# A tuned attention and mixer-MLP kernel: the second FFN product by seven block products, in groups of 256 tokens

## Chip, cores and metric

One core of a Trainium2 chip. The metric is device time in microseconds (us). Fast runs of the kernel before, on one chip, differ by up to 1.4 per cent here (265.68 to 269.4 in one set); short stretches at half TensorE clock, which the traces show, are at least part of the reason. Medians are over all runs, slow ones included (one of four in runs 8, 13 and 15, two of four in runs 1 and 7, three of four in run 14). Ratios are the mean time of one kernel's fast runs over the mean of the other's fast runs of the same rounds, so they are not quite the ratios of the medians quoted beside them. Faster or slower needs 2 per cent.

## The reference, cut to what matters

Block attention (4 batches, 8 heads, 768 tokens, 64 numbers a head; keys and values are first mixed over blocks by a matrix) gives `x` of 768 x 512 for each batch. Then a token-mixing and a channel-mixing layer follow:

```python
a1 = alpha1 * x + beta1
tok = np.einsum('ts,bsd->btd', w_tok, a1)
u = x + lam * tok
a2 = alpha2 * u + beta2
ch = np.maximum(a2 @ w_ch1, 0.0) @ w_ch2     # 512 -> 2048 -> 512
return u + lam * ch
```

`w_ch2` is called W2 below, and `np.maximum(...) @ w_ch2` is the second FFN product. `lam` is a vector over the 512 output channels.

## The kernel before

A batch is worked in two halves of 384 tokens. For each half the first product (`h_ps`) goes in 16 pieces, then the second (`ch_ps`) in three tiles of 128 tokens. While one half multiplies, the attention of the next batch is slotted between the pieces, by a table of places. Each engine gets its work in the order in which the program writes it. Some words of this text: the *affine* is `alpha * x + beta` ahead of a mixing layer (tiles `a` and `a2T`); *turned* means transposed by TensorE (`qt_ps`, then `qT`); *tails* are copies into the last 32 rows of a tile of 128 tokens, as a block has 96; a *pitch* is the time from one matmul's start to the next one's; the *return* is the reading back of values into `Vs`.

```python
def h_part(b, hf, m, cis):
    ...
        h_of[m] = psb([128, 384], FT, "h_ps")          # one of 4 PSUM buffers
    ...
        act.activation(hT_of[(b, hf)][m], h_of[m][:], AF.Relu)

def ch_unit(b, hf, kk, part=(0, HT)):
    ...
    for m in range(*part):                             # 16 matmuls of 512 columns
        pe.matmul(cps[:, 0:w], hT[m][:, kk * 128:(kk + 1) * 128], W2p[:, m, 0:w], ...)
    ...
    dve.tensor_tensor(ost[:], cps[:], lamB[:], ALU.mult)
    (dve if b == B - 1 and hf == 1 else pool).tensor_tensor(ost[:], ost[:], u_of[b][kt], ALU.add)
    act_out(out[b, kt * 96:(kt + 1) * 96, :], ost[0:96, :])

def moe_tok(b, kt, ps):                                # lam here: two operations on VectorE, one on GpSimd
    ...
    dve.tensor_tensor(tmp[:], tok_of[(b, kt)][:], lamB[:], ALU.mult)
    dve.tensor_tensor(u16_of[b][:, kt, :], tmp[:], x_of[b][:, kt, :], ALU.add)
    (pool if b else dve).tensor_tensor(u32[kt], tmp[:], x_of[b][:, kt, :], ALU.add)
```

The values of a later batch are mixed, written to memory (`vscr`) and read back in another order into `Vs`; there were two `Vs` buffers.

The softmax here doesn't subtract the row's maximum and nothing guards it: scores larger than these inputs give would overflow.

## Time and profile before

| | before |
|---|---|
| time, median of 3 | 265.45 us (265.23 to 265.5) |
| profiled run | 268.76 us, span 267.0, with 10.2 us at half clock from 22.8 us on |
| busy: TensorE, VectorE, ScalarE, GpSimd | 96, 57, 50, 38 per cent |

The profiled run is 3.3 us longer than the timed ones. It has one stretch at half clock in the head, which ends at 33 us. I take this for the cause, so from there on its places in time lie some 3.3 us later than in a typical run. The prediction shows the page's lines. The one view of before that it does not show is the timeline of GpSimd at 72 us (start, duration, engine, operation, count, idle time ahead of it and what ended that), which also belongs here:

```profile
74.54 1.26 POOL L65 TENSOR_TENSOR ost<-ost,u 128x512 f32<-128x512 f32 x1 [1.18 <-DVE ost L65]
75.75 1.11 POOL L65 DMA_DIRECT2D raw<-in_v_dram  x2
```

GpSimd issues batch 2's loads (`raw`, values first) only after its third add of `u` to an output tile.

### The profile page before, as it was taken

What the parts mean: (1) busy time and instruction counts of PE and PEld (TensorE: products, weight loads), DVE (VectorE), ACT (ScalarE), POOL (GpSimd) and SP (SyncE); (2) the same over time, 40 slices, a digit from 0 to 9 for tenths busy, and PEclk for the clock granted to TensorE, in tenths of its full rate; (3) what the DMA queues carried; (4) which work ended last, traced back from release to release, by engine and by line L of the source; (5) the groups of instructions that cost most, each with busy time, mean ns of one, the idle gap of its engine ahead of it and who ended that gap; (6) DMA issues with size and microseconds to landing.
All of it is one profiled execution on the core that took longest, in us unless ns stands there. A gap on an engine that the chain in (4) does not pass through costs nothing.

```text
span 267.0 us, 5344 instructions
## 1 busy us (share of the span) xinstructions
PE 256.0 (96%) x2148; PEld 142.7 (53%) x2164; DVE 151.4 (57%) x333; ACT 133.0 (50%) x238; POOL 100.8 (38%) x109
## 2 busy tenths in 40 slices
PE   8987899999999999999999999999999999999993
PEld 3465766454655545555465455555565445545552
DVE  5767567797729995434978453415794554121032
ACT  3675457344497539565257189474363014505600
POOL 8882600901184055629610444601301746031000
PEclk9997599999999999999999999999999999999998
DMA  6999999996959976996994348911110332112012
GB/s 99 204 210 196 206 206 214 169 143 150 147 120 202 136 137 148 148 140 121 177 166 91 60 96 185 153 24 39 43 39 0 61 90 68 21 39 79 0 42 79
DMA packets 67368, 31.03 MB, mean 116 GB/s; under 512 B 56640, under 2 KB 63056, under 8 KB 67344
## 3 DMA queue, kind: packets, MB, share of 16 engines
q0 software_dynamic: 26352, 15.34, 41.3%
q1 hardware_dynamic: 40896, 15.29, 30.3%
q8 instruction: 17, 0.28, 0.4%
q10 hardware_dynamic: 96, 0.07, 0.1%
q14 instruction: 7, 0.06, 0.1%
HBM read 32.78 MB, written 8.65 MB: 155 GB/s over the span
## 4 chain that ended last, share of the span: by engine, by line
PE 82%; DMA 6%; DVE 5%; POOL 2%; issue 2%; ACT 1%; SPq 0%; DVEq 0%; ACTq 0%; POOLq 0%
PE h_ps L65 29%; PE ch_ps L65 27%; PE tok_ps L65 12%; PE x_ps L65 4%; DMA v<-in_v_dram 3%; DMA out_dram<-ost 3%; PE sc_ps L65 3%; DVE a L65 2%; PE v_ps L65 2%; PE kmix_ps L65 2%; PE mix_ps L65 1%; DVE ost L65 1%; PE wtok_ps L65 1%; POOL vd L65 1%; DVE Vs L65 1%
## 5 line engine op out<-in xcount | busy, mean ns | idle before, releaser
L65 PE MATMUL h_ps<-a2T,W1p 128*128 128x384 bf16 x512 | 92.0, 326 | 0.4 <-DVE ost L65 0.3
L65 ACT ACTIVATE hTa<-h_ps 128x384 bf16<-128x384 f32 x96 | 46.7, 493 | 54.6 <-PE h_ps L65 54.4
L65 PE MATMUL ch_ps<-W2p,hTa 128*128 128x512 bf16 (+1 forms) x285 | 67.5, 370 | 0.8
L65 PEld LDWEIGHTS <-W1p 128*128 128x128 bf16 x512 | 48.3, 98 | 32.7 <-issue 0.8
L65 POOL TENSOR_TENSOR ost<-ost,u 128x512 f32<-128x512 f32 x21 | 26.6, 1267 | 77.3 <-DVE ost L65 59.2
L65 DVE TENSOR_TENSOR ost<-ch_ps,lamB 128x512 f32<-128x512 f32 (+1 forms) x25 | 16.7, 669 | 50.3 <-PE ch_ps L65 47.1
L65 PEld LDWEIGHTS <-hTa 128*128 128x128 bf16 x300 | 28.4, 98 | 28.9
L65 POOL TENSOR_TENSOR u<-toktmp,x 128x512 f32<-128x512 f32 x18 | 29.6, 1650 | 33.7 <-DVE toktmp L65 33.7
L65 ACT ACTIVATE et<-sc_ps 96x768 f16<-96x768 f32 (+1 forms) x32 | 25.0, 810 | 21.2 <-PE sc_ps L65 21.2
L65 PE MATMUL tok_ps<-a,w_tokT 128*128 128x512 f16 x126 | 30.3, 379 | 0.1
L65 ACT CAST kT<-kmix_ps 64x512 f16<-64x512 f32 x32 | 22.9, 717 | 10.1 <-PE kmix_ps L65 9.8
L65 DVE TENSOR_TENSOR toktmp<-tok_ps,lamB 128x512 f32<-128x512 f32 x21 | 14.5, 690 | 21.1 <-PE tok_ps L65 21.1
L65 PE MATMUL ch_ps<-W2p,hTb 128*128 128x512 bf16 (+1 forms) x99 | 24.6, 371 | 0.1
L65 PEld LDWEIGHTS <-w_tokT 128*128 128x128 f16 x126 | 12.3, 98 | 14.0 <-DVE a L65 0.5
L65 ACT ACTIVATE hTb<-h_ps 128x384 bf16<-128x384 f32 x32 | 15.7, 490 | 7.5 <-PE h_ps L65 7.2
L65 DVE TENSOR_TENSOR u<-toktmp,x 128x512 f16<-128x512 f32 (+1 forms) x24 | 17.0, 718 | 0.7
L65 POOL DMA_DIRECT2D qn<-in_q_dram x18 | 16.0, 929 | 3.5 <-DMA raw<-in_v_dram 3.5
L65 DVE TENSOR_TENSOR x<-x_ps,rcb 96x512 f16<-96x512 f32 x24 | 16.5, 687 | 0.8
L65 DVE TENSOR_SCALAR a2T<-uT,ab2col 128x384 bf16<-128x384 f16 x28 | 9.7, 409 | 11.2 <-DMA uT<-u 9.1
L65 PEld LDWEIGHTS <-et 96*128 96x128 f16 (+4 forms) x288 | 13.0, 106 | 5.3 <-issue 1.2
L65 PE MATMUL x_ps<-Vs,et 96*128 96x65 f16 (+4 forms) x288 | 14.2, 203 | 1.3 <-ACT et L65 0.9
L65 PEld LDWEIGHTS <-hTb 128*128 128x128 bf16 x100 | 9.5, 98 | 9.7
(114 smaller groups left out, 235.7 us busy)
## 6 DMA issues: line engine op xcount, KB each, us to landing
out_dram<-ost SPq DMA_DIRECT2D x23, 192.0 KB, 2.4
raw<-in_v_dram POOLq DMA_DIRECT2D x6, 384.0 KB, 7.6
raw<-in_k_dram POOLq DMA_DIRECT2D x6, 384.0 KB, 9.1
qn<-in_q_dram POOLq DMA_DIRECT2D x18, 128.0 KB, 10.0
vscr<-mixed SPq DMA_DIRECT2D x6, 384.0 KB, 4.6
Vs<-vscr SPq DMA_DIRECT2D x3, 768.0 KB, 7.9
W1p<-in_moe_w_ch_dram POOLq DMA_DIRECT2D x4, 512.0 KB, 13.0
W2p<-in_moe_w_ch_dram POOLq DMA_DIRECT2D x4, 512.0 KB, 14.1
```

Source lines behind the costliest of these rows:

```text
L65: ins = getattr(self.eng, name)(*args, **kwargs)
```

## The change

The intent: seven products of half-size blocks in place of eight (Strassen's scheme) save an eighth of the second product's matmul columns. For this, tokens go in three groups of 256, so that the hidden matrix splits into 2 x 2 blocks; W2 and the hidden values become fp16; VectorE makes four sums of hidden blocks per group and, once, four sums of W2's blocks; a product is accumulated over others in PSUM and copied out in between by ScalarE. The token affine carries `lam` (times 1024), so token mixing needs one VectorE operation. `Vs` has one buffer. The core of the diff, cut:

```diff
-            hTa = moep.tile([128, 12, 384], BF, name="hTa", tag="hTa", bufs=1)
+            hT_of[(b, g)] = moep.tile([128, HP, 2, GS], F16, name="hT", tag="hT", bufs=1)   # GS = 256
...
+    def sums(b, g, lo, hi, which):              # VectorE: 88 operations of 128x512 fp16 in all
+            dve.tensor_tensor(S[n], *((A[1][0], A[1][1]), (S[0], A[0][0]), (A[0][0], A[1][0]), (A[0][1], S[1]))[n], ...)
...
+        if n == 0:
+            product(b, g, 1, range(HP - 1))     # each product: 8 matmuls of 256 columns
+            product(b, g, 2, range(3))
+            product(b, g, 1, range(HP - 1, HP))
+            act.copy(o0[:, lo_c], a())
+            sums(b, g, 4, HP, (0, 1))
+        elif n == 1:
+            product(b, g, 2, range(3, HP))
+            dve.tensor_tensor(o0[:, lo_c], o0[:, lo_c], half(0), ALU.add)
+            sums(b, g, 4, HP, (2, 3))
+        elif n == 2:
+            product(b, g, 6, range(HP))         # accumulates on product 1: waits for the copy
+            act.copy(o0[:, hi_c], a())
+        elif n == 3:
+            product(b, g, 5, range(HP))
+            act.copy(ch_of["r"][:], half(1))
...                                             # products 7, 3, 4 likewise
+            dve.tensor_tensor(o[:, c], o[:, c], lamB[:, c], ALU.mult)
+            (dve if last else pool).tensor_tensor(o[:, c], o[:, c], u_of[(b, kt)][:, c], ALU.add)
...
-        dve.tensor_tensor(tmp[:], tok_of[(b, kt)][:], lamB[:], ALU.mult)
-        dve.tensor_tensor(u16_of[b][:, kt, :], tmp[:], x_of[b][:, kt, :], ALU.add)
-        (pool if b else dve).tensor_tensor(u32[kt], tmp[:], x_of[b][:, kt, :], ALU.add)
+        dve.scalar_tensor_tensor(u, tok_of[(b, kt)][:], 1.0 / LIFT, x_of[b][:, kt, :], op0=ALU.mult, op1=ALU.add)
+        act.copy(u16_of[b][:, kt, :], u)
...
-    Vs = [const([128, H * NB, GRP], F16, f"Vs_{n}") for n in range(2)]
+    Vs = const([128, H * NB, GRP], F16, "Vs")
```

The table of places was written anew for groups of 256; the very first group stays plain.

## The prediction

> **What bounds the kernel now.** I read the page first: the busy shares, then the slices.
>
> ```profile
> PE 256.0 (96%) x2148; PEld 142.7 (53%) x2164; DVE 151.4 (57%) x333; ACT 133.0 (50%) x238; POOL 100.8 (38%) x109
> ...
> PE   8987899999999999999999999999999999999993
> ...
> PEclk9997599999999999999999999999999999999998
> ```
>
> TensorE is at 9 tenths in nearly every slice from the sixth on, and its clock is whole except in slices four and five (20 to 33 us). A busy TensorE is not yet a full one, since neighbouring matmuls overlap in the record, so I took the pitch from the timeline of TensorE alone, near the end, where nothing else is mixed in (start, duration, count):
>
> ```profile
> 231.13 2.75 PE L65 MATMUL ch_ps<-W2p,hTa 128*128 128x512 bf16 x11
> ...
> 241.49 10.56 PE L65 MATMUL h_ps<-a2T,W1p 128*128 128x384 bf16 x64
> 251.89 2.75 PE L65 MATMUL ch_ps<-W2p,hTa 128*128 128x512 bf16 x11
> ...
> 258.80 1.47 PE L65 MATMUL ch_ps<-W2p,hTa 128*128 128x256 bf16 x12
> ...
> 261.85 0.60 PE L65 MATMUL ch_ps<-W2p,hTb 128*128 128x256 bf16 x4
> ```
>
> From start to start: 48 matmuls of 512 columns (one record is missing) in 241.49 - 231.13 = 10.36 us, 215.8 ns each; 64 of 384 in 10.40 us, 162.5 ns; 28 of 256 in 3.05 us, 108.9 ns. Each is columns / 2.4 GHz plus 2 to 3 ns. So the long stages run at the matmul pitch and not at a wait. To see how much waiting hides between them I summed these pitches, and those of the small attention matmuls (16 scores 0.45 us, 16 value products 0.51 us), over 73.5 to 262.4 us: 185.5 of 188.9 us. Only some 3.4 us are slack there. The chain that ended last says the same (82% TensorE), and the list of TensorE's own waits adds to under 6 us, nearly all before 30 us. What shortens this kernel is fewer matmul columns; what lengthens it is a wait that TensorE does not have today.
>
> **What the Trainium skill says.**
> - "TensorE: Matmul & The Clock Gate", section "Wait — 56ns, not 53.3ns?": a warm start-to-start gap is N / 2.4 GHz plus about 2.5 ns per matmul. The three pitches above agree. The price of smaller matmuls is thus 2.5 ns each.
> - The same page, "Step-by-step: what each phase is for": the next weight load is pulled ahead and runs beside the current matmul. The trace agrees: a load is 98 ns long and 256 columns still go at 108.9 ns. 98 under 109 is close, but 128-column products of `kmix_ps` go at 56 ns with a new weight each, so the loads do not set the pitch.
> - "VectorE: DVE Perf Modes", "What auto-detection actually checks": a tensor_tensor whose tensors are all 16-bit may take two elements a cycle. Here 128x768 in fp16 takes 550 to 558 ns, while 128x512 from PSUM in fp32 takes 690. The new fp16 sums are priced from the former.
>
> **The change, part by part.**
>
> *Matmul columns.* The first product keeps its columns but goes from 512 matmuls of 384 to 768 of 256: 83.2 to 83.6 us, +0.4. The second product has 368 of 512 and 32 of 256 before: 79.4 + 3.5 = 82.9 us. After, the first group of 256 tokens is plain (32 of 512) and eleven groups take seven products of eight matmuls of 256: 32 x 215.8 + 616 x 108.9 = 6.9 + 67.1 = 74.0 us, -8.9. Of the ideal eighth of 82.9 us, 10.4, the plain group keeps 0.9 and the short matmuls 0.6. Token mixing: six more of 512 for the third tile of the first batch, +1.3; the 24 that mix the first tokens of that batch shrink from 384 to 256 columns, -1.3. Turning back, row sums and transposes of that first tile lose 2816 columns, -1.2. Sum: **-9.7 us**. About 2300 of the lost columns lie at 30 to 34 us, where matmuls run at half pace (24 value products take 1.62 us there, 1.02 a little later): at most another -1.0; I take -0.5.
>
> *VectorE.* Added: per group four sums of two 128x512 pieces in fp16. From 476 and 421 ns for 96x512 I take 0.42 each: 88 x 0.42 = 37 us. Output combining goes from 29 small and large operations (about 19 us) to some 71 (about 33). Weight sums: four of 128x2048, about 1.2 each, once. Removed: moe_tok had two operations of 0.69 and 0.72 per 128 tokens and gets one, because lam now sits in the token affine: -15. The affine runs on full tiles after the tails are copied, not on 96 rows followed by copies of both tensors: -11. Net 151 to about 180 us, 70% of the span.
>
> *ScalarE.* Relu goes from 128 x 0.49 to 96 of 512 columns; the line through 384 (0.493) and 768 (0.807) gives 0.60: 62 to 57 us. Added: 44 PSUM copies of 256 at about 0.39 and 22 half-precision copies of u at 0.6: +30. Casts that move from VectorE add a few. Net 133 to about 163.
>
> *GpSimd* loses 18 additions of 1.65 us and gains three in the head. None of it is on the path.
>
> *Buffers.* One value buffer is enough if the next batch's values are fetched after the last value product of this one; by the order of instructions they are, by a whole group. The second w_tok staging no longer blocks the key load of batch 1:
>
> ```profile
> 46.80 1.03 POOL L65 DMA_DIRECT2D raw<-in_k_dram  x2 [15.22 <-ACT hTa L65]
> ```
>
> That wait of GpSimd goes away, but the keys were needed only at 63 us, now at some 56. It allows the shorter first group and yields nothing itself.
>
> *New waits.* TensorE's order in a group is products 1, 2, 6, 5, 7, 3, 4, and 1, 6, 7, 4 accumulate in the same bank with a copy of it taken in between. Product 6 may start only when ScalarE has copied product 1. After product 1 there are five matmuls of product 2, 0.54 us; drain, hand-over and copy are 0.17 + 0.05 + 0.39 + 0.05 = 0.66 (estimates from the 272 ns of one 256-column matmul less its pitch, and the copy from ScalarE's line). So 0.1 to 0.2 us per group, in the seven or so groups where no attention is slotted in: +1.2. Before products 7 and 4 another product of 0.87 us covers the copy. The sums for product 6 are ready about 1.7 us after the last first-product matmul; sixteen matmuls take 1.74: no wait, unless VectorE lags. It does so most in the second group of batch 0 and after it, where eight normalisations of 0.89, the sums and 2.8 us of tails and affine meet: 18 us of VectorE against 17 of TensorE. I allow +1.0 there, and +0.5 for the first group, which also holds the weight sums.
>
> *The end.* Before: last matmul's end at 262.45, then
>
> ```profile
> 262.99 0.42 DVE L65 TENSOR_TENSOR ost<-ch_ps,lamB 128x256 f32<-128x256 f32 x1 [1.36 <-DMA out_dram<-ost]
> 263.45 0.42 DVE L65 TENSOR_TENSOR ost<-ost,u 128x256 f32<-128x256 f32 x1
> ```
>
> so 1.4 us to the last store. After: the buffer wait is gone, but nine operations of 0.42 queue on VectorE during products 3 and 4 and end some 2.1 us after product 4: +0.7.
>
> Sum: -9.7 - 0.5 + 1.2 + 1.5 + 0.7 = -6.8. Against this, some of today's 3.4 us go: at 137 us TensorE waits for an output buffer, and around 127 us the chain runs through the affine that is removed. -0.9. Total -7.7, **257.7 us**.
>
> **The rivals.**
> 1. *The gain is given back to VectorE and ScalarE.* At 70% and 64% with strict orders, each group could wait 0.5 to 1 us for a sum, a copy, or a bank. For it: the four PSUM banks rotate over first-product tiles, both product accumulators and token mixing, so a late release of an accumulator stops the third and fourth tile of the next group. Against it: tiles two and three come 1.7 us later, and outside batch 1 the engines have a third of their time free. It would make 261 to 265.
> 2. *The short matmuls do not hold 109 ns*, because weights now come from strided sums or differ on every matmul. For it: 98 ns of weight load against 109. Against: the last quarter output of today has just this form. At 115 ns, 1384 matmuls would cost 8.4 us: no gain.
> 3. *The tuned slots hide everything.* The steady slack stays at 3.4 us or shrinks and product 6 finds its copy in time: the ledger alone, -10.2, gives 255.
>
> **Range and chances.** The ledger's -10 is firm, as its pitches are measured in this kernel; the 2 to 3 us of waits are the uncertain part, and could as well be 0 as 6. Hence 257.7, with 254.3 to 261.5 as the range. The line of 2% is 265.45 x 0.98 = 260.1. The middle lies 2.4 us under it and the upper tail crosses it if the waits reach twice my sum: faster 0.75, same 0.23, slower 0.02.
>
> **What would show each step.** 256-column matmuls of both products at 109 ns start to start: the ledger; at 115 or more, rival 2. TensorE's waits at product 6 on a ScalarE copy of 0.1 to 0.2 us in groups without attention; if they are 0.5, or stand before sums, rival 1. VectorE busy about 180 us, ScalarE 163. The second group should begin about 7 us earlier than the 73.5 us at which the second half begins now. The last store should follow the last matmul by 2 us. Wrong altogether if the granted clock fell outside the head, or if the first group waited for W2 or batch 1's values.

## The result, and the profile after

The changed kernel takes 269.3 us (median of 4 runs, 269.13 to 270.24) against 265.48 (one of its four runs, 269.76, counts as slow and is not in the ratio): ratio 1.0154, 95% interval 1.0124 to 1.0185. It is slower by 1.5 per cent, within the 2 per cent that count as the same, and outside the forecast range.

The page after, the same lines as the prediction shows of before:

```profile
PE 247.3 (92%) x2665; PEld 189.0 (71%) x2665; DVE 180.3 (67%) x419; ACT 157.2 (59%) x278; POOL 77.8 (29%) x94
...
PE   8986999797899998999999999999997999999992
...
PEclk9999999999999999999999999999999999999997
```

VectorE's 180 us are as forecast, ScalarE's 157 are 6 under the forecast 163. TensorE works 8.7 us less by this line, and there are three sevens in its slices after the first 40 us, where before has none. The timeline of TensorE near the end gives the pitch of the new matmuls:

```profile
235.75 7.15 PE L69 MATMUL h_ps<-a2T,W1p 128*128 128x256 bf16 x64
242.74 0.93 PE L69 MATMUL cha_ps<-W2p,hT 128*128 128x256 f16 x7
...
245.48 1.04 PE L69 MATMUL chb_ps<-W2p,hs 128*128 128x256 f16 x8
246.35 1.04 PE L69 MATMUL cha_ps<-T,hs 128*128 128x256 f16 x8
```

64 of them start over 6.99 us, 109.2 ns each; eight with weights from sums over 0.87 us, 108.8 ns. The short matmuls hold their pace.

To find the time I took all matmuls in the order of their starts, from the first hidden product to the last matmul, and set each distance against the pitch of the earlier one (columns / 2.4 GHz + 2.4 ns; 28 and 32 ns for scores and value products). What is over is waiting (what is under is taken off). A distance of a whole number of pitches within one tile counts as a lost record or half clock, not as waiting. Some lost records at the edge of a tile put about 1 us of matmul time of before into its waiting.

| us | before | after | difference |
|---|---|---|---|
| first hidden product (before less the 3.3 us above) | 35.9 | 34.7 | -1.2 |
| matmul time from there to the last matmul | 216.7 | 210.7 | -6.0 |
| waiting in the first 40 us of it | 3.0 | 6.5 | +3.5 |
| waiting in the rest | 3.3 | 10.1 | +6.8 |
| from the last matmul's end to the end | 4.5 | 5.3 | +0.7 |
| sum | | | +3.8 |

The sum is the measured difference. So the saving came, and 10 us of waiting took more than all of it. TensorE's waits from 34 us on, first before (all), then after (the six largest of ten lines; the others have 0.2 to 0.4 us each); us in total, times, longest:

```profile
PE kmix_ps L65 <- DVE sel L65: 0.3, 1, 0.3
PE h_ps L65 <- DVE ost L65: 0.3, 1, 0.3
```

```profile
PE h_ps L69 <- ACT qT L69: 2.2, 1, 2.2
PE tok_ps L69 <- DVE a L69: 2.0, 2, 1.6
PE mix_ps L69 <- DMA raw<-in_v_dram: 1.6, 1, 1.6
PE h_ps L69 <- DVE a2T L69: 1.5, 3, 1.0
PE cha_ps L69 <- ACT ost L69: 0.7, 2, 0.4
PE x_ps L69 <- DMA Vs<-vscr: 0.6, 1, 0.6
```

They are a few single waits, each for another producer. None of these lines names a sum of hidden blocks (`hs`). Two of them have a visible history. The first, on TensorE and then on ScalarE:

```profile
63.86 1.03 PE L69 MATMUL h_ps<-a2T,W1p 128*128 128x256 bf16 x8
64.73 0.50 PE L69 MATMUL qt_ps<-ident,qn 128*128 128x128 f16 x6
67.47 1.03 PE L69 MATMUL h_ps<-a2T,W1p 128*128 128x256 bf16 x8 [2.24 <-ACT qT L69]
```

```profile
63.70 2.89 ACT L69 CAST kT<-kmix_ps 64x512 f16<-64x512 f32 x4
66.62 1.50 ACT L69 COPY qT<-qt_ps 128x768 f16<-128x768 f16 x2
```

The next hidden piece needs one of the four PSUM buffers, and the one whose turn it is still holds turned queries of batch 1, which ScalarE copies only after 2.9 us of key casts. The second group starts at 63.9 us, the second half before at 73.5 (70 in a typical run): batch 1's attention has come forward into the stretch where its loads arrive and its keys are cast.

The other is the wait of `tok_ps` for the affine `a` at 204 us. VectorE and GpSimd just before it:

```profile
200.93 0.42 DVE L69 TENSOR_TENSOR ost<-cha_ps,lamB 128x256 f32<-128x256 f32 x1
201.26 1.16 DVE L69 TENSOR_TENSOR ost<-ost,lamB 128x256 f32<-128x256 f32 x1
202.45 1.86 DVE L69 COPY x<-x 32x512 f16<-32x512 f16 x3
204.34 0.96 DVE L69 TENSOR_TENSOR a<-x,alphaB 128x1536 f16<-128x1536 f16 x1
```

```profile
200.81 1.33 POOL L69 TENSOR_TENSOR ost<-ost,u 128x512 f32<-128x512 f32 x1 [12.95 <-DVE ost L69]
202.55 1.31 POOL L69 TENSOR_TENSOR ost<-ost,u 128x512 f32<-128x512 f32 x1 [0.41 <-DVE ost L69]
```

A 128x256 multiplication takes 0.42 us when one operand is in PSUM and 1.16 us when both are in SBUF and GpSimd is adding. It ends 0.28 us after GpSimd's add. Run 9 below has no adds on GpSimd, and there the same operations go:

```profile
199.99 0.42 DVE L69 TENSOR_TENSOR ost<-ost,lamB 128x256 f32<-128x256 f32 x1
200.44 0.89 DVE L69 COPY x<-x 32x512 f16<-32x512 f16 x3
```

The two together are 0.74 + 0.97 = 1.7 us longer in the changed kernel, which is nearly the whole of the 1.8 us that TensorE waits behind them. The Trainium skill, "SBUF — State Buffer", section "Who interferes with whom", says that a VectorE instruction with two SBUF inputs contends with a GpSimd instruction that reads SBUF, that copies in fast modes do too, and that the one that comes first holds the shared ports for its whole instruction. The traces agree: 0.42 beside 1.16 us, three copies in 1.86 beside 0.89 us, and the multiplication's end just after the add's.

### The profile page after: what moved, and what is told of

Its sections match the earlier page's. It is cut to its first block, busy times and chain, and to the rows that moved or that the text cites. A ratio compares the mean times of both kernels' runs of the same rounds, so it can differ in the third digit from the quotient of the medians.

```text
span 267.6 us, 6547 instructions
## 1 busy us (share of the span) xinstructions
PE 247.3 (92%) x2665; PEld 189.0 (71%) x2665; DVE 180.3 (67%) x419; ACT 157.2 (59%) x278; POOL 77.8 (29%) x94
## 4 chain that ended last, share of the span: by engine, by line
PE 57%; DVE 15%; DMA 12%; ACT 8%; issue 4%; POOL 2%; SPq 0%; ACTq 0%; DVEq 0%; POOLq 0%
PE h_ps L69 19%; PE cha_ps L69 12%; PE chb_ps L69 8%; PE tok_ps L69 8%; DMA raw<-in_v_dram 6%; DVE ost L69 4%; ACT kT L69 4%; DVE x L69 4%; DMA Vs<-vscr 3%; DMA v<-in_v_dram 3%; PE x_ps L69 3%; DVE a L69 3%; PE sc_ps L69 2%; PE v_ps L69 2%; DVE a2T L69 1%
## 5 line engine op out<-in xcount | busy, mean ns | idle before, releaser
L69 PE MATMUL h_ps<-a2T,W1p 128*128 128x256 bf16 x768 | 93.2, 273 | 3.7 <-ACT qT L69 2.2
L69 PEld LDWEIGHTS <-W1p 128*128 128x128 bf16 x768 | 73.6, 98 | 17.0 <-issue 4.3
L69 ACT ACTIVATE hT<-h_ps 128x512 f16<-128x512 f32 x96 | 56.1, 601 | 24.7 <-PE h_ps L69 23.5
L69 PEld LDWEIGHTS <-hs 128*128 128x128 f16 x352 | 33.5, 98 | 5.5 <-issue 1.0
L69 PEld LDWEIGHTS <-hT 128*128 128x128 f16 x296 | 28.3, 98 | 7.3 <-ACT hT L69 0.5
L69 DVE SCALAR_TENSOR_TENSOR u<-tok_ps,x 128x512 f32<-128x512 f32 x22 | 15.2, 691 | 26.9 <-PE tok_ps L69 26.5
L69 DVE TENSOR_TENSOR hs<-hT 128x512 f16<-128x512 f16 x44 | 18.4, 419 | 19.2 <-ACT hT L69 19.2
L69 PE MATMUL cha_ps<-T,hs 128*128 128x256 f16 x176 | 22.8, 272 | 0.7 <-ACT ost L69 0.7
L69 PEld LDWEIGHTS <-w_tokT 128*128 128x128 f16 x132 | 12.7, 98 | 15.0 <-DVE a L69 2.9
L69 PE MATMUL chb_ps<-W2p,hs 128*128 128x256 f16 x176 | 22.8, 273 | 0.0
L69 POOL DMA_DIRECT2D qn<-in_q_dram x18 | 16.0, 900 | 12.7 <-DMA raw<-in_v_dram 5.7
L69 DVE TENSOR_TENSOR ost<-ost,lamB 128x256 f32<-128x256 f32 (+1 forms) x23 | 18.3, 794 | 0.4
```

The costliest lines, as they stand in the source:

```text
L69: ins = getattr(self.eng, name)(*args, **kwargs)
```

## The experiments

Theory A at the start: the waits are single placements in the engines' orders and can be mended one by one. Theory B: the seven products bring them by their work on VectorE and ScalarE. Later came C (GpSimd's adds slow VectorE) and D (batch 2's loads slow the return of batch 1's values). "Waiting" below is the pair (first 40 us / rest) of the table above, 6.5 / 10.1 in the changed kernel. It is read from one profiled run each, so I weigh it more than times, which half-clock stretches blur. "Fast ratio" is against the kernel before on the same chip.

**1. No seven products.**

```diff
-            for n in range(7 if b or g else 8):
-                (ch_step if b or g else ch_plain)(b, g, n)
+            for n in range(8):
+                ch_plain(b, g, n)
```

and no `sums`, no `weights`.

> Every group's second product is made block by block (64 matmuls of 256 columns in place of 56), with no sums and no weight sums on VectorE; groups of 256, the token affine with lam and the single value buffer stay. Theory A (the loss is one-off waits from where things stand in the engines' orders; the seven products themselves pay): 11 groups x 8 matmuls x 108.9 ns = 9.6 us more TensorE, less the product-6 waits (about 1.6 us) and those waits that stand behind the sums on VectorE (some 2 to 4 us): 274 us, range 272 to 277. Theory B (the seven products bring the waits, so that without them all goes away): the 11 us of extra waiting go with them and the time comes back to 268 or less.

Measured: 275.71 us median (271.68 to 278.26), fast ratio 1.0264 (1.0154 to 1.0374), so about 1.1 per cent over the changed kernel's; with two fast runs, the interval is too wide for the time alone to show it. Waiting 6.1 / 2.5. From 34 us on TensorE has left:

```profile
PE h_ps L69 <- ACT qT L69: 2.2, 1, 2.2
PE mix_ps L69 <- DVE sel L69: 0.8, 1, 0.8
PE h_ps L69 <- ACT hT L69: 0.3, 1, 0.3
PE h_ps L69 <- DVE a2T L69: 0.3, 1, 0.3
```

So the waits of the first 40 us are not the seven products': they come with what this run keeps, the groups of 256 with their new table of places, the single value buffer and the affine with lam (which of these, no run separates). Of the 10.1 us after it 7.6 do come with them. That leaves theory B for the rest, and A for the first stretch at most. The expectation has the matmuls wrong: a plain group runs as 32 matmuls of 512 columns and not as 64 of 256, so the seven products save 11 x (32 x 215.8 - 56 x 108.9 ns) = 8.9 us, not 9.6. Less 7.6 of waits that leaves 1.3 us; the two ratios give 1.1 per cent, 2.9 us.

**2 to 4. Three single placements.**

```diff
+    load_kv(1, (1,))                 # run 2: batch 1's values ahead of W2; keys stay
-    for n, at_ in enumerate((("c", 2), ("c", 4), ("c", 6))):
+    for n, at_ in enumerate((("c", 0), ("c", 2), ("c", 4))):                    # run 3: keys' casts
-        put(p, 2, "c", 5 if b == 1 else 4, lambda b=b: moe_affine(b, 0))
+        put(p, 2, "c", 4, lambda b=b: moe_affine(b, 0))                         # run 4
```

> Only batch 1's values are fetched ahead of the loads of W2; all else as in the changed kernel. Theory A: the wait of the value mixing of batch 1 for its values (1.76 us in the changed kernel's trace) and the wait for the values' return from memory behind it (0.74 us) go, and the time falls by 2.5 us to 266.8; at least 1.2 us. Theory B (waits on the values are beside the sums' and would be replaced by the next wait): under 0.7 us.

> Only the three casts of batch 1's keys on ScalarE stand two steps earlier in the last group of batch 0. Theory A: the 2.4 us wait of the first product for qT, which stands in ScalarE's queue behind these casts, goes: -2.0 to -2.4 us, 267. Theory B: ScalarE is short of time there whatever the order, and the wait comes back at another place: under 0.7 us.

> Only the affine of the next batch's first group stands at step 4 instead of 5 of batch 1's preceding group. Theory A: the four waits of the first product for a2T at 104.9 to 106.9 us (0.41 + 1.11 + 0.15 + 0.15 = 1.8 us) go: -1.5 to -1.8 us. Theory B: VectorE is full there by the sums and the wait only moves: under 0.5 us.

Measured: values first 270.1 us (1.012, waiting 6.0 / 10.2); keys early 273.07 (1.0224, 8.2 / 10.7); affine earlier 269.5 (1.013, 6.1 / 9.6). Theory A fails for each: the intervals of values first (1.0066 to 1.0174) and affine earlier (1.0068 to 1.0193) take in the changed kernel's 1.0154, and keys early (1.016 to 1.0288) is not below it. With the values there early, the mixing waits 0.95 us for its matrix from VectorE. With the keys cast early, TensorE waits 1.6 us for keys that have not landed and 3.2 us for the values' return from memory. With the affine earlier, 1.2 us of wait appear at 112 us. In all three a mended wait uncovers another.

These runs also show half-clock windows. The granted clock in 40 slices of the span, first of run 2, then of run 3:

```profile
PEclk9997999999799999999999999999999999999998
```

```profile
PEclk9999799999979999999999999999999999999998
```

The second dip of each is one window of 3.4 us that starts at 69.3 and 75.3 us, 1.6 and 0.6 us after a wait of 2.4 and 3.2 us has ended. Of the 20 traces, 17 have a wait of 2.39 us or more after 34 us, and 12 of them have such a window (of 3.4 to 10.2 us) within or just after it; the three without such a wait (before and the last two runs) have none. In run 7, 3.4 us at half clock also follow two waits of 0.9 and 1.5 us with one short matmul between them (60.5 to 63.1 us). Where TensorE has no slack, 3.4 us at half clock cost half their length, 1.7 us by estimate.

**5 to 8. What in the seven products: sums, lam, GpSimd's adds; and all placements.** The first three give a wrong result on purpose.

```diff
-        for n in which:
-            dve.tensor_tensor(S[n], ...)
+        for n in ():                                  # run 5: products take blocks of hT for the sums
-            dve.tensor_tensor(o[:, c], o[:, c], lamB[:, c], ALU.mult)           # run 6: out, twice
-            pool.tensor_tensor(o1[:], o1[:], u_of[(b, kt + 1)][:], ALU.add)     # run 7: out, and its likes
+    # run 8, all in one: values ahead of W2; keys' casts at c1, c3, c5; affine at c4;
+    # half_done(b, 1) at (p, 1, "c", 4); mix_matrix(3) at h2; product(b, g, 2, range(2)) first
```

> A wrong result on purpose: the four products that take sums of hT take blocks of hT in their place, so that VectorE makes none of the 88 sums (36.9 us of its time); matmuls, copies, finishing and GpSimd's adds are all kept. Theory B (the sums fill VectorE by stretches, and what stands behind them in its order comes late to TensorE): the waits after 66 us that the block-by-block kernel did not have either, 7.7 us less the product-6 waits of some 1.6 us, go: 263 us, range 261 to 265. Theory A (single placements, only the one at 116 us stands behind sums): at most 1.5 us less, 268 or more.

> A wrong result on purpose: the multiplication of the finished rows by lam is left out in the seven-product groups but for the one that empties product 4's accumulator (23 operations, 18.2 us of VectorE), sums and GpSimd's adds are kept. Theory B with VectorE's whole load as the cause: about the same relief for half the work taken away, 2 to 4 us less. Sums alone as the cause (their place in the order, not the load): under 1 us less.

> A wrong result on purpose: GpSimd's 23 adds of u to the output rows are left out (the last group's adds on VectorE stay), nothing is put in their place. If GpSimd's adds stretch what VectorE does beside them (the 128x256 multiplications by lam had a mean of 873 ns, against 416 to 425 for others of that size): that group comes back to about 425 ns, the token-mixing wait of 1.8 us at 204 us falls by over 1 us, and the time falls by 1 to 3 us. If that stretching costs nothing on the path: under 0.7 us.

> All placements mended together, result right: batch 1's values fetched ahead of W2, its keys' casts at steps 1, 3, 5 (not 0, 2, 4: there the keys had not landed), the next batch's first affine at step 4, the token affine's second half at step 4 of the group before, the fourth mixing matrix at step 2, product 1's last matmul after two of product 2. Theory A: the named waits go one by one, -2.0 for keys and values, -1.8, -2.3, -0.9: about 262. Theory B: the waits behind VectorE only move; 0 to 3 us less, 266 to 269.

| run | time, us | fast ratio | waiting |
|---|---|---|---|
| changed kernel | 269.3 | 1.0154 | 6.5 / 10.1 |
| no sums | 267.95 | 1.0059 (1.0031 to 1.0088) | 6.5 / 8.7 |
| no lam in finishing | 266.27 | 1.0005 (0.9958 to 1.0051) | 5.2 / 7.1 |
| no adds on GpSimd | 282.24 | 1.0598 (1.0536 to 1.0659) | 13.5 / 7.2 |
| all placements | 267.73 | 1.0034 (0.9989 to 1.0079) | 5.6 / 8.0 |

The sums, the largest part of the new work on VectorE (37 us), are worth 1.4 us of waiting. The 18 us of finishing multiplications are worth 3.0. So it is not VectorE's load in sum. My reading: the finishing operations stand at the border of two groups, ahead of the affine, the tails and the normalisations that TensorE needs next; the sums stand where it has other work. Without GpSimd's adds the rest of the waiting falls by 2.9 us, but a wait of 9.1 us for the values' return from memory appears at 74 us. GpSimd, which has nothing to add, issues batch 2's loads of values at 55 us and of keys at 66.1 (changed kernel: 66.6 and 67.7); the return is issued at 67.8 us and not at 63.9, and takes 15.4 us and not 8.8. My expectation had no word of that. The placements together gave 1.6 us by the medians, 3.2 by the ratios, and not the 7 of theory A.

**9 to 12. The adds without that side effect, the adds moved, and lam put into W2.**

```diff
+        if b == 2:                                    # all four: GpSimd waits for the second group's first hidden piece
+            pool.tensor_copy(gate[:], hT_of[(0, 1)][0:1, 0, 0, 0:1])
-            (dve if last else pool).tensor_tensor(o[:, c], ...u..., ALU.add)    # run 9: out
+            dve.tensor_tensor(o[:, c], ...u..., ALU.add)                        # run 10: on VectorE
+        dve.tensor_tensor(w, w, lamL[:]..., ALU.mult)                           # runs 11, 12: W2 *= 1024 lam, once
+        act.activation(o0[:, lo_c], a(), AF.Copy, scale=1.0 / LIFT)             #   copies scale back
+        dve.scalar_tensor_tensor(o, half(1), 1.0 / LIFT, ..., op0=ALU.mult, op1=ALU.add)
```

> A wrong result on purpose, as the run without GpSimd's adds, but batch 2's loads, which the adds held back until 66.6 us, are held by a GpSimd copy of one number that the first product of the second group makes (67 us). Theory C (GpSimd's adds slow what VectorE does beside them, and the late results are what TensorE waits for): the 9.1 us wait for batch 1's values at 74 us goes back to 0.7, the waits at 105 and 204 us stay away, and the waiting between the first hidden product and the last matmul falls from 16.7 us by 4 to 5: 264.5 to 265.5 us. If the adds were not the cause of those waits: 268 or more.

> Right result: the same 23 adds of u stand on VectorE instead of GpSimd (23 x 0.69 = 15.9 us more of VectorE's own time), loads of batch 2 held as in the run before. Theory C: what VectorE takes over is about what it loses to GpSimd's adds, and no operation is stretched any more; the time falls by 0.5 to 3 us, 266.5 to 269. Theory B (VectorE's load by itself brings the waits): 1 to 4 us slower than the changed kernel, 270.5 or more.

> Right result: W2 is multiplied by lam (times 1024) once, four operations of 1.22 us on VectorE in the first group; every finishing multiplication by lam goes, u is added by VectorE in operations that it makes anyway or in one of 0.69 us, and GpSimd adds nothing. Loads of batch 2 held as above. Theory C: VectorE's time falls by about 10 us and nothing is stretched: 3 to 5 us less than the changed kernel, 264.5 to 266.5, if the four scalings cost the first group nothing; each microsecond that they cost there is added. Theory A alone: 1 us less at most.

> Right result: the same with the mended placements, the sums of W2 for product 7 and 4 two steps later, batch 1's value casts on ScalarE and two copies of qT and a half of the last keys' casts on VectorE. If A and C are both true and add up: the all-placements run's gain of 2 us and the gain of lam in W2 of 3 to 5 us: 262 to 264, the first right version that beats the kernel before. If both remove the same waits: 265 or more.

| run | time, us | fast ratio | waiting |
|---|---|---|---|
| no adds, loads held | 265.97 (264.59 to 266.1) | 0.9939 (0.9858 to 1.002) | 6.0 / 6.3 |
| adds on VectorE | 270.36 | 1.0125 (1.0053 to 1.0196) | 6.1 / 10.8 |
| lam in W2 | 268.92 | 1.0052 (0.998 to 1.0124) | 7.2 / 8.6 |
| lam in W2, placements | 268.29 | 1.0041 (0.9979 to 1.0104) | 7.0 / 9.1 |

Run 9 confirms C: with the loads held the 9.1 us wait is gone, and the rest of the waiting falls from 10.1 to 6.3. (That is 3.8 us where 4 to 5 were expected. By its times alone it is level with the kernel before; the interval reaches 1.002.) The finishing multiplications in the groups of instructions (busy us, mean ns), after and in run 9:

```profile
L69 DVE TENSOR_TENSOR ost<-ost,lamB 128x256 f32<-128x256 f32 x13 | 11.3, 873 | 0.1
```

```profile
L69 DVE TENSOR_TENSOR ost<-ost,lamB 128x256 f32<-128x256 f32 x13 | 5.4, 418 | 0.1
```

The 1.8 us wait at 204 us and the 1.1 us one at 105 us have gone too. (Taking the adds out also lets output rows be stored sooner; no run separates that from the stretching, but at 204 us the two timelines above leave it 0.1 us at most.) Run 10 says that it is no gain to give the adds to VectorE: 15.2 us of work of its own (22 adds of 692 ns in its trace, where the expectation counted 23) cost what the stretching cost. What counts is the time that finishing takes from VectorE, by whichever way. Runs 11 and 12 cut that work, but I had given VectorE the emptying of product 5's accumulator, and product 3 waited 0.8 us for it at 144 us and at 200 us in run 11 (142 and 200 in run 12); and the wait at 65 us was still there (2.4 and 3.1 us, with half-clock windows of 6.8 and 3.4 us). They came out 2 to 6 us worse than expected, run 12 where its rival put it (265 or more).

**13 to 16. The wait at 65 us, ScalarE's bursts, and the worth of the seven products.**

```diff
-    for g, at_ in enumerate(((0, "c", 5), (0, "c", 6), (0, "c", 7), (1, "h", 0))):
-        put(0, *at_, lambda g=g: q_turn_late(1, g, act.copy))
+    for g, at_ in enumerate(((0, "c", 6), (0, "c", 7), (1, "h", 4), (1, "h", 6))):   # runs 13 to 16; weights(2), (3) at h2, h3
+        put(0, *at_, lambda g=g: q_turn_late(1, g, dve.tensor_copy if g < 2 else act.copy))
+    def k_cast(b, n, engs, par):      # runs 14 to 16: two casts now, two a step later
+            act.activation(ch_of["r"][:], half(1), AF.Copy, scale=1.0 / LIFT)        # run 15: as 12, product 5 by ScalarE
```

> The changed kernel with only batch 1's query turning moved: the first two of its four pieces one step later and copied by VectorE, the last two in the second group (steps 4 and 6), and the two later sums of W2 to steps 2 and 3 of that group. Theory: the 2.4 us wait at 65 us is four PSUM buffers held by pieces that ScalarE copies only after its bursts of key casts. It falls under 0.8 us: -1.6 to -2.4 us, and the half-clock window of 3.4 us that followed this wait in most runs on this chip (68 to 72 us) does not come: up to 1.7 us more. 265.5 to 267.7. Rival: ScalarE has too much to do there whatever the order, and the wait comes back within a few steps: under 0.8 us less.

> The all-placements version with that, and every burst of four key casts on ScalarE (2.9 us) cut into two of 1.45 us in neighbouring steps. Right result. Theory (bursts on ScalarE longer than the four PSUM buffers of a 256-token step can bridge): besides the wait at 63 us those at 111 us (1.28) and 144 us (0.99) go: 2.5 to 4 us less than the all-placements run (267.7): 263.5 to 265.5. Rival (each wait comes back elsewhere): 266.5 or more.

> The same with lam in W2 and no adds on GpSimd, product 5's result copied by ScalarE as in the changed kernel (the 0.8 us waits at 144 and 200 us of the two versions with lam in W2 came of VectorE reading it). Right result. Theory C (less work on VectorE and none beside it on GpSimd frees 3.6 to 4 us of the waiting after 66 us): 1 to 3 us less than the version before, 262 to 264. Rival: the waits that it takes are the same ones: within 0.7 us of it or slower.

> The same placements as two runs before, but every group's second product block by block (88 matmuls of 256 columns more, 9.6 us). It tells what the seven products are worth where the other waits are mended. Theory C: they bring some waiting of their own (product 6 on ScalarE's copy, GpSimd's adds beside VectorE's shorter pieces), 3 to 5 us, so this is 5 to 7 us slower than its seven-product twin: 270 to 272. If the seven products brought nearly no waiting: 9 us slower; if they brought as much as they save: equal.

Measured: queries late 271.38 us (1.0151; waiting 7.0 / 10.1). The wait at 65 us fell to 0.6 us, and 3.0 us for the values' return came at 69 us: the rival was right about the sum, the theory about the cause. Run 14, bursts cut, had three of four runs slow (273.73 to 273.94, one fast run of 265.52) and so no ratio. Its profile is of a slow run. It shows what made that run long, TensorE at 69 us and GpSimd ahead of it; the other two slow runs, within about 0.2 us of it, were not traced, nor was the fast one:

```profile
68.75 0.50 PE L69 MATMUL qt_ps<-ident,qn 128*128 128x128 f16 x6
78.02 0.62 PE L69 MATMUL x_ps<-Vs,et 96*128 96x65 f16 x8 [8.77 <-DMA Vs<-vscr]
```

```profile
63.32 1.26 POOL L69 TENSOR_TENSOR ost<-ost,u 128x512 f32<-128x512 f32 x1 [4.78 <-DVE ost L69]
64.53 1.09 POOL L69 DMA_DIRECT2D raw<-in_v_dram  x2
```

The return is issued at 63.1 us and batch 2's loads 1.5 us later; it takes 14.8 us. The mended order had let VectorE, and so GpSimd, finish a little earlier. Of the two waits that cutting the bursts was to remove, the one at 144 us is gone in this profile; in place of the one at 111 us stands one of 1.1 us at 117. Run 15: 266.0 us (0.9961, 0.9901 to 1.0022), within the rival's range if run 14's one fast run is the measure; its profile fell in a slow run. There ScalarE's copy for product 6 waits for an output row to be stored, and product 6 for it, 2.4 us at 140 us. Run 16, the plain twin of run 14: 278.84 us (278.51 to 279.02), and its profile has the same 8.9 us wait, which the expected 270 to 272 did not reckon with. Against the three slow runs of 14 (273.9), one of which is known to have that wait, it is 5.0 us slower. The two profiles agree: the first 40 us wait alike, the rest 7.7 us in run 14 and 3.5 in run 16, and 8.9 of matmuls less these 4.2 is 4.7. So the seven products are worth about 5 us where the placements are mended. This is an estimate from runs that share one long wait; by fast runs alone it is not shown, as run 14 has one.

**17 and 18. The return of the values held free, and everything together.**

```diff
+        if b == 2:
+            pool.tensor_copy(gate[:], Vs[0:1, 0, 0:1])      # both: batch 2's loads after the return has landed
-  name="ost", tag="ost", bufs=2
+  name="ost", tag="ost", bufs=4                             # run 18, with run 15's edits and batch 3's key casts a step earlier
```

> The kernel with only batch 1's query turning moved (3.0 us of waiting for the values' return from memory at 69 us, landed at 72.3), and one thing more: GpSimd issues batch 2's loads only when that return has landed. Theory D (the return takes 8.8 us because batch 2's loads, 2.3 MB, are issued 2 to 3 us after it begins and share the DMA engines; in the kernel before, GpSimd's later adds held them until 75.8 us, after the return): the return lands in 5 to 6 us, by 69.5; the wait at 69 us falls under 0.7 us; no half-clock window follows; 2 to 4 us less than that run's 271.4: 267.5 to 269.5 on this chip. If the return is slow for itself: it lands at 72 again, batch 2's loads are 5 us later, and the time is the same or up to 4 us worse.

> The version with lam in W2, no adds on GpSimd, mended placements, with the values' return held free of batch 2's loads, four output row buffers in place of two (product 6 waited 2.4 us for ScalarE, and that for a store, at 140 us) and batch 3's key casts one step earlier. Right result. The three waits (2.45 at 70, 2.56 at 140, 1.2 at 152) had cost 6.2 us in the slow profile of that version and some less in its fast runs (265.65 us): 261.5 to 264.5, over 0.5 per cent less than the kernel before. If they only move: 265 to 267.

Measured: run 17 has 268.75 us (1.0089, 1.0042 to 1.0135; waiting 5.0 / 10.0) beside 271.38 (1.0151) of run 13. The return takes 7.6 us, not 8.8, and lands at 71.6; the wait is 1.8 us, not 3.0, and no half-clock window follows in its profile. Theory D is right in direction, and about half the size that I expected (the intervals of the two ratios overlap, so it rests on the traces). The return's length against the start of batch 2's loads, over the runs:

| kernel | return issued | loads of batch 2 | return took |
|---|---|---|---|
| before | 66.6 | 9.1 us later | 6.9 us (end of its last packet) |
| run 17 | 64.0 | after it | 7.6 us (6.9 to its last packet) |
| run 18 | 66.7 | after it | 7.9 us (7.0) |
| changed | 63.9 | 2.7 us later | 8.8 us (7.1) |
| run 13 | 63.5 | 2.2 us later | 8.8 us (7.2) |
| run 14 | 63.1 | 1.5 us later | 14.8 us (14.4) |
| no adds on GpSimd | 67.8 | values 12.7 us, keys 1.7 us earlier | 15.4 us (14.3) |

The trace's records of packets show why 0.7 us decides so much. In run 14 the first packets of the loads (6 KB each) start at 68.4 us, when some 1400 of the return's 6144 packets (128 bytes each) have not; the return falls from about 1100 packets started in a microsecond to 40, and ends when the loads end, at 77 us. In run 13 the loads' first packets start at 69.7 us, when some 270 are left, and the last packet ends only 0.3 us later after its issue than in run 17; the rest of the difference between 8.8 and 7.6 us lies between the last packet and the signal of landing.

Even alone the return does not reach the 69 us at which TensorE now wants it, so a floor of some 2 us stays unless it starts earlier. Before, the values were there at 73.5 and wanted at 77.3.

Run 18: 265.38 us (263.79 to 267.06 in 6 runs), fast ratio 0.9955 (0.9906 to 1.0003). It is level with the kernel before (half a per cent better at the mean, with an interval that takes in no difference), and 2 per cent below the changed kernel's ratio. Its waiting is 5.9 / 6.8, with these three as the largest of nine lines:

```profile
PE x_ps L69 <- DMA Vs<-vscr: 1.7, 1, 1.7
PE mix_ps L69 <- DVE sel L69: 1.2, 1, 1.2
PE x_ps L69 <- DVE x L69: 0.8, 1, 0.8
```

The expected 261.5 to 264.5 was not reached at the median; it is where the rival (the waits only move, 265 to 267) put it. Its remaining waits are again single ones.

## Why the prediction was wrong

The count of matmul columns held. What failed is the term for new waits, +1.2 + 1.5 - 0.9 = +1.8 us of the prediction's sum, by two steps. One took batch 1's attention, wanted about 7 us earlier, to cost at most the +0.5 of the first group, after a check of the keys alone. The other took nothing of GpSimd's work to be "on the path", and the other engines to "have a third of their time free". In place of 1.8 us the traces show 10 us more waiting (12 with the lost records put right), 3.5 of it in the first 40 us. Step by step:

- *Matmul pitch and the column ledger*: right. 108.8 to 109.2 ns where 108.9 was forecast; rival 2 is out. From the first hidden product on, -6.0 us by the method above, and about -7.5 if five lost records of the second product before (1.1 us, above in its waiting) and half a microsecond of pitches counted too many after are put where they belong. The forecast's +0.4 and -8.9, with +1.0 of token mixing in this stretch, give -7.5 as well.
- *The head*: what is left of the forecast's -10.2 for it is -2.7, and -1.2 came. The half-clock stretch at 23 to 33 us, from which -0.5 was to come, was not the kernel's: the timed runs of before are 3.3 us shorter than the profiled one, and the profiled run after does not have it.
- *VectorE 180, ScalarE 163*: right for VectorE (180.3), 6 us too much for ScalarE (157.2).
- *Second group about 7 us earlier*: right (63.9 against some 70).
- *Product 6 and ScalarE's copy, +1.2*: right in kind; six waits of 0.12 to 0.60 us at product 6 and two of 0.13 at product 1's last matmul, 1.7 us. *Sums: no wait*: nearly right, 1.4 us in the run without them. *The end, +0.7*: right.
- *"The second w_tok staging no longer blocks the key load ... yields nothing itself"* and "one value buffer is enough": true as far as it goes, but the step that failed first is beside it. Groups of 256 call for batch 1's attention some 6 us sooner, and I checked only that keys had time. The values were late (1.6 us of wait in the first group; the prediction names this as the sign that it is "wrong altogether"), their return was late, and ScalarE's bursts stood before the turned queries. The first 40 us wait 3.5 us more, with or without the seven products.
- *"GpSimd loses 18 additions ... None of it is on the path"*: false, twice. GpSimd's adds stretch VectorE's operations beside them and are worth 3.8 us of waiting after the first 40 us. And their place in GpSimd's order had timed batch 2's loads: before, the third add held them until after the values had returned; in the changed kernel they run into its end (a wait of at most 0.7 us there, 8.8 us in run 14).
- *"Outside batch 1 the engines have a third of their time free"*: this argument against rival 1 is the main fault. An average share says nothing of the microseconds at a group's border. There some 3 us of finishing stand ahead of the tails and the affine (199.6 to 202.4 us in the example), and the wait falls there. Rival 1 was the nearest (261 to 265), though not by the sums that I had in mind, and still 4 us short. *"Some of today's 3.4 us slack goes, -0.9"*: it grew.
- In the sum of the prediction the term "new waits, +1.2 + 1.5 - 0.9" should have been about +10: 3.5 in the first 40 us, where the attention comes earlier, and 6.8 from finishing on VectorE, GpSimd's adds and product 6. The split of the 6.8 does not add up exactly, as the causes overlap (lam 3.0, adds 3.8, sums 1.4, product 6 some 1.7).

What stays open: why a wait of 2.4 us is followed by half clock in one run and not in another; which part of the change outside the seven products (groups, table, value buffer) brings the waits of the first 40 us; and whether a rewritten table of places could take the 12.7 us of waiting of run 18 to the 6.3 of the kernel before. Only that would make the change a clear gain.

## What to carry to other kernels

When a change makes the pieces of the busiest engine shorter, price the waits at the borders, not the average shares: list what each other engine must finish between the last piece of one group and the first of the next, in its own order. Ask what a removed or moved operation had been holding back in its queue; the transfers behind it will now start earlier and may run into one that matters. And judge a mended wait by the sum of all waits, because the next one may be waiting just behind it.

## What the Trainium skill lacked or had wrong

- "TensorE: Matmul & The Clock Gate", section "HAM oscillation — how this bites in real kernels": it puts the limit at a gap of about 3.4 us without matmuls. Here waits of 2.39 to 2.45 us were followed by half clock in six traces (3.4 us in five, 6.8 in one; run 2: wait at 65.3, half clock from 69.3 to 72.7), and by none in four others. The three traces whose longest wait after 34 us is 1.8 us or less have no half clock after 34 us but at their very end.
- "SBUF — State Buffer", section "Who interferes with whom": borne out, and the page gives no time for this pair. The runs show it: VectorE's 128x256 fp32 multiplication from SBUF had a mean of 873 ns beside GpSimd's adds and 418 without, and its twin with one operand in PSUM 416 with them.
- "DMA: Bandwidth & Descriptors" and the other pages give no time that a strided read of small rows loses to another transfer. The return of 768 KB in rows of 128 bytes took 7.6 and 7.9 us alone, 8.8 us when 2.3 MB of loads were issued 2.2 or 2.7 us behind it, and 14.8 us at 1.5 us behind.
